# Weight loads on two queues at a written pace, K^T loads behind V, and a planner that lets instruction blocks wait for loads

## Chip, cores and metric

One core of one Trainium2 chip runs the kernel. The metric is the device time of a run in microseconds (us). Three runs of the kernel before gave 1008.52, 1013.25 and 1024.26 us (median 1013.25).

## What is computed

A delta-rule attention (4 batches, 8 heads, 768 positions, head size 48) feeds two mixture layers with 2048 hidden columns. Cut to what matters:

```python
k_n = k / (norm(k) + 1e-6)
for t in range(S):
    y[t]  = q[t] @ state
    v_old = k_n[t] @ state
    state = state + beta[t] * outer(k_n[t], v[t] - v_old)
h = x @ w_in;  g = P(h) / (Q(h) + 1e-6);  x = g @ w_out      # P cubic, Q quadratic in |h|
h = x @ w2_in; r = maximum(h, 0);         out = (r * r) @ w2_out
```

## The kernel before

The 768 positions are cut into 12 chunks of 64; a chunk of one batch is a step, eight steps are a group, and there are six groups. A group needs its Gram matrices (TensorE, line 583), the inverse of a triangular matrix, made row by row over 31 steps (lines 652 and 656: on VectorE for group 0, on GpSimd for the others), and then per step small matmuls (lines 793, 835, 841). The steps of group 0 are written apart: `halves` does the lower and upper 32 rows of a chunk (L835), with a cross product between them (L841), and `rest` makes outputs and the state (L793).

The 3072 tokens are cut into six tiles of 512. For every tile and each of 16 blocks of 128 hidden columns, `mm1` (L1128) makes h, `rational` the quotient, and `mm2_1` (L1216, or L1219 where the operands are split in two) adds g @ w_out. The second layer (`relu2`, `mm2_2`, L1249 to L1251) follows when all tiles are done. Tile 0 can start when group 0 has left its output; the later groups run between the matmuls of the tiles before.

The weights arrive as 768 KB blocks `src[j]`, 16 of them per layer, in 64-bit words. ScalarE (L1052, L1053), VectorE (L1069 to L1075) and again ScalarE, VectorE or GpSimd (L1086, L1088) turn each into 32-bit operands `A` and `B`. Blocks 0 to 3 land in `mem`, blocks 4, 5, 8 and later in two buffers `raw`, blocks 6 and 7 in `ra`. All loads are asked for by SyncE's queue (SP), from the helper `dma` (L399), in program order.

TensorE's clock is kept up early on by matmuls that compute nothing: `fill` (L513). A first run of six, one of 24 behind the first weight block (`gate`, L1064), and 13 spare ones of three that the planner sets where it thinks TensorE too idle.

What stands where is decided by a planner (`Plan`). Every piece of work is a task with an engine, a duration, a due time, and a time `nb` before which it is not started in the plan. `play` runs all tasks through a model of the engines, and `search` shakes the due times at random and keeps a set that brings more TensorE work forward. The finished order is then written out; the chip follows order and semaphores, and no time of the plan is in the program. So any change of a cost shifts the whole order, also where the cost does not apply.

The planner counts TensorE's instructions in blocks of 256 (`BLOCK`; `SENT` is where the count starts). When TensorE enters a block, the next one is fetched, and in the plan TensorE can't go into that one until a time `FETCH` later (L203):

```python
if e == "PE" and sent + t["ins"] > BLOCK:
    s = max(s, turn + FETCH[turn > 80] - t["dur"] * (BLOCK - sent) / t["ins"])
```

with `FETCH` 4.7 us up to 80 us of the plan and 3.0 us behind. A DMA occupies SP for `iss`, lands `lat` after its bytes have gone through at 240 KB per us (L254 to L257), and the program's semaphores let each DMA wait until the eighth one before it has landed.

## Time and profile before

| | |
|---|---|
| runs | 1008.52, 1013.25, 1024.26 us |
| the profiled execution | 1007.86 us |
| its span in the profile | 1006.1 us, so 1.8 us lie around it |
| TensorE busy | 972.7 us (97%) |
| VectorE, ScalarE, GpSimd busy | 676.8, 622.4, 498.8 us |
| granted TensorE clock, mean | 0.985 |

Line numbers (L1128) are those of the kernel. PE is TensorE's matmuls, SPq the DMA queue of SyncE; times start with the span. A row of the timeline has start, length, engine, line, operation and, in brackets, how long the engine sat idle before and what ended that. "issue" as the releaser means that the profile shows nothing that was waited for.

### The profile page before, as it was taken

How to read it: one execution, taken by the hardware profiler on the slowest of the kernel's cores; microseconds unless marked ns; L12 is line 12 of the kernel's file. 1: busy time of each engine (PE TensorE's matmuls, PEld its weight loads, DVE VectorE, ACT ScalarE, POOL GpSimd, SP SyncE). 2: the span in 40 equal slices, each digit the busy share in tenths (PEclk: the TensorE clock that was granted, in tenths of full speed). 3: DMA queues.
4: the chain of work that ended last, by engine and by line, in shares of the span. 5: the costliest groups of instructions: out<-in, count | busy, mean ns of one | idle time of the engine just before them, and what ended most of it. 6: DMA issues, size and time to landing. Idle time of an engine off the chain costs nothing.

```text
span 1006.1 us, 23661 instructions
## 1 busy us (share of the span) xinstructions
PE 972.7 (97%) x9682; PEld 776.1 (77%) x9682; DVE 676.8 (67%) x1097; ACT 622.4 (62%) x1129; POOL 498.8 (50%) x619
## 2 busy tenths in 40 slices
PE   5799999999989999999999999999999999999998
PEld 4678666678768778887888888888888888888886
DVE  7867877988897799779879998753333433334332
ACT  5557876988787688688769887652332333423322
POOL 4287389999999979975437977520000000000000
PEclk8779999999999999999999999999999999999999
DMA  7883875334343541333121227210010100000000
GB/s 195 235 261 99 166 227 132 85 78 122 77 100 78 150 102 47 83 95 58 29 77 53 69 94 288 94 53 11 1 64 0 32 32 1 32 1 1 32 1 32
DMA packets 127149, 85.14 MB, mean 85 GB/s; under 512 B 95616, under 2 KB 112000, under 8 KB 127040
## 3 DMA queue, kind: packets, MB, share of 16 engines
q1 hardware_dynamic: 127040, 83.62, 29.8%
q8 instruction: 76, 1.25, 0.5%
q14 instruction: 33, 0.27, 0.1%
HBM read 64.00 MB, written 18.61 MB: 82 GB/s over the span
## 4 chain that ended last, share of the span: by engine, by line
PE 77%; POOL 13%; DVE 5%; issue 2%; ACT 1%; DMA 1%; SPq 1%; POOLq 0%; DVEq 0%; ACTq 0%
PE bank L1128 33%; PE bank L1219 13%; PE bank L1251 7%; PE bank L1249 7%; PE bank L1250 7%; PE bank L793 6%; POOL mem L1167 3%; POOL Tt L656 3%; POOL tmp L652 3%; POOL pl L1190 2%; PE bank L1216 2%; PE bank L513 2%; DVE tmp L652 1%; DVE Tt L656 1%; SPq L399 1%
## 5 line engine op out<-in xcount | busy, mean ns | idle before, releaser
L1128 PE MATMUL bank<-xh,A 128*128 128x512 f32 (+1 forms) x1170 | 366.2, 395 | 3.1 <-DVE mem L1172 2.1
L1128 PEld LDWEIGHTS bank<-xh,A 128*128 128x128 f32 x1170 | 216.4, 188 | 57.2 <-issue 4.3
L1128 PE MATMUL bank<-xl,A 128*128 128x512 f32 (+1 forms) x585 | 226.5, 387 | 0.1
L1237 DVE SCALAR_TENSOR_TENSOR mem<-bank,mem 128x512 f32<-128x512 f32 x96 | 66.3, 691 | 159.3 <-ACT mem L1236 159.1
L1236 ACT ACTIVATE mem<-bank 128x512 f32<-128x512 f32 x96 | 57.4, 598 | 159.7 <-PE bank L1128 159.7
L1167 POOL TENSOR_TENSOR mem<-mem 128x512 f32<-128x512 f32 x89 | 116.3, 1308 | 53.0 <-ACT mem L1159 48.6
L1128 PEld LDWEIGHTS bank<-xl,A 128*128 128x128 f32 x585 | 109.9, 188 | 24.2 <-DVE xl L1112 0.9
L1251 PE MATMUL bank<-gh,C 128*128 128x512 f32 x288 | 113.7, 395 | 0.0
L1249 PE MATMUL bank<-gl,C 128*128 128x512 f32 x288 | 113.4, 394 | 0.0
L1190 POOL TENSOR_TENSOR pl<-mem,ph 128x512 fp32r<-128x512 f32 x78 | 102.6, 1315 | 21.3 <-ACT ph L1189 17.2
L1250 PE MATMUL bank<-gh,C 128*128 128x512 f32 x288 | 112.1, 389 | 0.0
L1240 DVE TENSOR_TENSOR gl<-mem,gh 128x512 fp32r<-128x512 f32 x96 | 69.2, 723 | 62.3 <-ACT gh L1239 62.3
L1219 PE MATMUL bank<-pl,E 128*128 128x512 f32 x240 | 97.5, 406 | 4.5 <-POOL pl L1190 4.1
L1239 ACT CAST gh<-mem 128x512 fp32r<-128x512 f32 x96 | 59.6, 621 | 67.0 <-DVE mem L1237 51.8
L656 POOL TENSOR_TENSOR Tt<-Tt,tmp 128x31 f32<-128x31 f32 (+15 forms) x155 | 91.8, 592 | 8.9
L1219 PE MATMUL bank<-ph,F 128*128 128x512 f32 x240 | 93.7, 391 | 0.0
L1219 PE MATMUL bank<-ph,E 128*128 128x512 f32 x240 | 93.6, 390 | 0.0
L652 POOL TENSOR_TENSOR tmp<-Gb,Tt 128x31 f32<-128x31 f32 (+15 forms) x155 | 87.6, 565 | 11.8 <-DVE Gb L629 2.2
L1179 ACT ACTIVATE mem<-mem,par 128x512 f32<-128x512 f32 x96 | 69.4, 723 | 31.3 <-POOL mem L1167 30.0
L1170 DVE SCALAR_TENSOR_TENSOR mem<-mem,par,bank 128x512 f32<-128x512 f32 x96 | 71.3, 742 | 20.2 <-ACT bank L1180 19.9
L1155 ACT ACTIVATE mem<-bank 128x512 f32<-128x512 f32 x96 | 56.7, 592 | 33.1 <-PE bank L1128 27.7
L1168 DVE TENSOR_TENSOR mem<-bank,mem 128x512 f32<-128x512 f32 x96 | 65.8, 686 | 12.9 <-ACT mem L414 7.2
(203 smaller groups left out, 1798.4 us busy)
## 6 DMA issues: line engine op xcount, KB each, us to landing
raw<-in_w_dram SPq DMA_DIRECT2D x17, 768.0 KB, 5.6
rb<-in_w_dram SPq DMA_DIRECT2D x8, 768.0 KB, 5.0
gs<-Gs SPq DMA_DIRECT2D x40, 128.0 KB, 2.5
X<-in_qT_dram SPq DMA_DIRECT2D x44, 112.0 KB, 2.9
kn<-in_kn_dram SPq DMA_DIRECT2D x12, 384.0 KB, 4.6
vn<-in_vn_dram SPq DMA_DIRECT2D x12, 384.0 KB, 3.4
y<-mem SPq DMA_DIRECT2D x18, 256.0 KB, 2.3
out_dram<-mem SPq DMA_DIRECT2D x18, 256.0 KB, 2.0
```

Source lines behind the costliest of these rows:

```text
L652: E_.tensor_tensor(tv, _mid(Gb[:, s, s + 1:32], [128, a, b]), Tt[:, 0:a, s:s + 1].to_broadcast([128, a, b]), op=ALU.mult)
L656: E_.tensor_tensor(Tt[:, 0:a, s + 1:32], Tt[:, 0:a, s + 1:32], tv, op=ALU.subtract if g else ALU.add)
L1128: M.matmul(h, a, b, start=(k == m == 0), stop=(k == NK - 1 and m == 2))
L1167: shared(1.29, 0.7, lambda E: E.tensor_tensor(b(), b(), a(), op=ALU.mult), r=[ak], w=[bk], due=due + 4.2)
L1170: q3 = lambda: V.scalar_tensor_tensor(c(), c(), s(0), h(), op0=ALU.add, op1=ALU.mult)
L1179: add("ACT", 0.72, lambda: A_.activation(a(), b(), AF.Ln, bias=s(6)), r=[bk, "par6"], w=[ak], due=due + 6)
L1190: shared(1.3, 0.7, lambda E: E.tensor_tensor(slot[mk][0], g(), slot[pk][0], op=ALU.subtract), r=[gk, pk], w=[mk], due=due + 11.5, alloc=(( ...
L1219: M.matmul(acc[d], a, b, start=(j == 0 and m == 0), stop=(j == NJ - 1 and m == 2))
L1240: add("DVE", 0.7, lambda: V.tensor_tensor(gl(), b(), gh(), op=ALU.subtract), r=[bk, gk, "late"], w=[lk], due=due + 5, lock=1, alloc=(("gl" ...
L1249: M.matmul(acc[d], wh, gl, start=(j == 0), stop=False)
L1250: M.matmul(acc[d], wl, gh, start=False, stop=False)
L1251: M.matmul(acc[d], wh, gh, start=False, stop=(j == NJ - 1))
```

## The change

Weight blocks 5 to 11 of the first layer are asked for by ScalarE's queue (`by=1`), blocks 5 to 10 at new times `PACE`. K^T of steps 8 to 11 stands behind the load of V of chunk 2 instead of a time of 55. K, V of chunk 2 and Q of steps 8 to 11 may start at 50 in the plan instead of 60. In the planner one `FETCH` of 2.7 us holds throughout, and the fetch of a block begins only when all loads asked for until then are drained in the model (`dma`). The threshold for spare fills becomes 3000 before 50 us of the plan and 1950 after it, instead of 2050. The other edits let a DMA stand on ScalarE's queue.

```diff
-BLOCK, SENT, FETCH = 256, 63, (4.7, 3.0)
+BLOCK, SENT, FETCH = 256, 63, 2.7
+QA, QB = 5, 12
+PACE = {5: 52.5, 6: 57.5, 7: 63, 8: 68, 9: 73, 10: 80}
-FILL0, FILLS, FILLN, LOOK, HOT, SPAN, SWAP = 6, 16, 3, 2.6, 2050, (41.5, 82), 0.08
+FILL0, FILLS, FILLN, LOOK, HOT, SPAN, SWAP = 6, 16, 3, 2.6, (3000, 1950), (41.5, 82), 0.08
-                s = max(s, turn + FETCH[turn > 80] - t["dur"] * (BLOCK - sent) / t["ins"])
+                s = max(s, turn + FETCH - t["dur"] * (BLOCK - sent) / t["ins"])
-            if e == "SP":
+            if t["kb"] or e == "SP":
                 free_at[e] = s + t["iss"]
...
                         turn = end - t["dur"] * sent / t["ins"]
+                        turn = max(turn + 0.3, dma)
-    def dma(kb, out, in_, r=(), w=(), due=0.0, lat=2.2, **kw):
+    def dma(kb, out, in_, r=(), w=(), due=0.0, lat=2.2, by=0, **kw):
         def go():
-            SY.dma_start(out() if callable(out) else out, in_() if callable(in_) else in_)
-        return add("SP", lat, go, r, w, due, kb=kb, **kw)
+            (SY, A_)[by].dma_start(out() if callable(out) else out, in_() if callable(in_) else in_)
+        return add(("SP", "ACT")[by], lat, go, r, w, due, kb=kb, **kw)
...
-                dma(384, VN[cb], vn[c], ..., nb=(16, 24, 60)[min(c, 2)], ...)
+                dma(384, VN[cb], vn[c], ..., nb=(16, 24, 50)[min(c, 2)], ...)
+                if c == 2:
+                    used["vn2"] = len(PL.tasks) - 1
-                dma(112, lambda: slot["kc", n][0:112], kT[n, 0:112], ..., nb=55 if n < 12 else 0, ...)
+                dma(112, lambda: slot["kc", n][0:112], kT[n, 0:112], ..., after=[used['vn2']] if n < 12 else [], ...)
...
-            nb=0 if l == 2 else WB + WS * j)
+            nb=0 if l == 2 else PACE[j] if j in PACE else WB + WS * j, by=int(l == 1 and QA <= j < QB), iss=0.45 if l == 1 and QA <= j < QB else 0.35)
```

In the order that comes of it nearly every row stands elsewhere. Three places are shown; the line numbers of the kernel after are 3 to 5 higher at the same code.

SP's queue at the start asks for the first K blocks: `TT1` is K^T of the first half-heads and `TT0` the same with the halves swapped. Before:

```order
L399 DMA TT1_125<-in_kT_dram 112x2x256
L399 DMA TT0_124<-in_kS_dram 112x2x256
L399 DMA TT1_125<-in_kT_dram 112x2x256
L399 DMA TT0_124<-in_kS_dram 112x2x256
L399 DMA be_136<-in_beta_dram 128x32
```

and after:

```order
L402 DMA TT1_125<-in_kT_dram 112x2x256 x2
L402 DMA TT0_124<-in_kS_dram 112x2x256 x2
L402 DMA be_136<-in_beta_dram 128x32
L1017 DMA par_82<-in_par_dram 128x6
L402 DMA TT1_125<-in_kT_dram 112x2x256
```

The second and third load have changed places, so the first pair is complete one load later. VectorE's copies out of the Gram matrices that these loads feed, before:

```order
L505 COPY TT0_124<-bank3_72 32x2x128 x4
L505 COPY TT0_124<-bank4_73 32x2x128 x4
L593 STREAM_TRANSPOSE Gb0_127<-TT0_124 128x1024
L858 TENSOR_TENSOR X0_120<-bank0_69,tri_135 128x4x64
L858 TENSOR_TENSOR X1_121<-bank1_70,tri_135 128x4x64
```

and after:

```order
L508 COPY TT0_124<-bank4_73 32x2x128 x3
L508 COPY TT0_124<-bank3_72 32x2x128 x4
L508 COPY TT0_124<-bank4_73 32x2x128
L598 STREAM_TRANSPOSE Gb0_127<-TT0_124 128x1024
L863 TENSOR_TENSOR X1_121<-bank1_70,tri_135 128x4x64
```

Now the first copies read bank 4, which belongs to the last of the four loads; before, they read bank 3 of the first pair.

SP's queue from weight block 4 on (`raw0`), before, with block 5 (`raw1`), K^T of steps 8 to 11 (`kTc`), block 6 (`ra2`) and Q (`X`):

```order
L399 DMA raw0_106<-in_w1_dram 128x768
L399 DMA raw1_107<-in_w1_dram 128x768
L399 DMA kTc0_145<-in_kT_dram 112x256
L399 DMA kTc1_146<-in_kT_dram 112x256
L399 DMA kTc2_147<-in_kT_dram 112x256
L399 DMA kTc3_148<-in_kT_dram 112x256
L399 DMA ra2_893<-in_w1_dram 128x768
L399 DMA X0_120<-in_qT_dram 112x4x64
```

and after:

```order
L402 DMA raw0_106<-in_w1_dram 128x768
L402 DMA X0_120<-in_qT_dram 112x4x64
L402 DMA X1_121<-in_qT_dram 112x4x64
L402 DMA X2_122<-in_qT_dram 112x4x64
L402 DMA vn0_143<-in_vn_dram 128x768
L402 DMA X3_123<-in_qT_dram 112x4x64
L402 DMA kn0_141<-in_kn_dram 128x768
L402 DMA kTc0_145<-in_kT_dram 112x256
```

Blocks 5 and 6 have left the queue, and what follows block 4 are loads into buffers that a step of group 0 must free first. The same blocks on ScalarE, after, where `XQ0` and `SX0` are the state that the first step left and `X1`, `UX1` copies of the second step's values:

```order
L417 CAST xh_100<-bank4_73 128x3x64
L417 COPY SX0_116<-bank5_74 112x3x16
L417 COPY XQ0_108<-bank5_74 112x4x48
L1091 CAST A2_86<-B0_177 128x384
L417 COPY UX1_113<-bank6_75 128x3x16
L417 COPY X1_121<-bank6_75 128x4x48
L402 DMA raw1_107<-in_w1_dram 128x768
L417 COPY UX2_114<-bank7_76 128x3x16
L417 COPY X2_122<-bank7_76 128x4x48
```

Block 5 now stands behind the copies of the first step's results, so it can't be asked for before TensorE has made these; before, it was asked for directly behind block 4.

## Rows read from the trace of the kernel before

**Rows 1.** The page: busy time of each engine (share of the span).

```profile
PE 972.7 (97%) x9682; PEld 776.1 (77%) x9682; DVE 676.8 (67%) x1097; ACT 622.4 (62%) x1129; POOL 498.8 (50%) x619
```

**Rows 2.** Stretches, all engines: PE, PEld, DVE, ACT, POOL busy, PEclk, DMA share, GB/s.

```profile
55.00:60.00 5.00, 2.84 (x22) 1.82 (x23) 2.56 (x6) 1.97 (x4) 4.37 (x9) 0.77 1.11 260
60.00:65.00 5.00, 5.00 (x67) 4.30 (x67) 2.86 (x6) 2.15 (x6) 4.53 (x7) 0.50 0.40 64
```

**Rows 3.** The chain that ended last, 50 to 80 us: start, length, what.

```profile
54.78 2.38 issue
57.16 1.27 PE bank L793 x17
58.43 1.57 PE bank L513 x3
60.01 0.78 PE bank L835 x16
60.79 1.02 PE bank L841 x16
61.81 1.69 PE bank L793 x16
...
65.85 1.49 PE bank L793 x31
...
68.23 0.46 PE bank L835 x16
68.69 0.91 PE bank L793 x16
69.61 0.89 PE bank L513 x3
...
71.76 1.51 PE bank L793 x48
...
74.63 0.60 PE bank L841 x16
```

**Rows 4.** Stretches from 0, PE alone: length, busy, matmuls, PEclk, DMA share, GB/s.

```profile
0.00:50.70 50.70, 33.67 (x598) 0.80 0.80 217
0.00:55.00 55.00, 37.74 (x726) 0.81 0.82 229
0.00:119.00 119.00, 98.80 (x1745) 0.87 0.70 190
```

**Rows 5.** Timeline of SP's queue, 48 to 54 us.

```profile
48.49 1.00 SPq L399 DMA_DIRECT2D raw<-in_w_dram  x2
49.53 2.47 SPq L399 DMA_DIRECT2D kTc<-in_kT_dram  x4
52.04 0.43 SPq L399 DMA_DIRECT2D ra<-in_w_dram  x1
```

**Rows 6.** DMA queues, 54.5 to 55 us: packets, MB, share of 16 engines.

```profile
DMA packets 139, 0.18 MB, mean 357 GB/s; under 512 B 20, under 2 KB 130, under 8 KB 138
...
q8 instruction: 1, 0.02, 12.2%
```

**Rows 7.** Timeline of TensorE, 5 to 45 us.

```profile
7.10 1.15 PE L491 MATMUL bank<-TT 48*64 48x64 f32 x60 [0.36 <-DMA TT<-in_kS_dram]
...
44.12 0.67 PE L841 MATMUL bank<-X,xin 32*64 32x48 f32 x16 [0.82 <-POOL A L1088]
```

**Rows 8.** Timeline of VectorE, 5 to 12 us.

```profile
6.65 3.47 DVE L505 COPY TT<-bank 32x256 f32<-32x256 f32 x8 [3.02 <-PE bank L491]
10.35 1.94 DVE L593 STREAM_TRANSPOSE Gb<-TT 128x1024 f32<-128x1024 f32 x1 [0.23 <-ACT TT L507]
```

**Rows 9.** What TensorE waited for from 84 us on: total, times, longest.

```profile
PE bank L1219 <- POOL pl L1190: 4.1, 6, 1.9
...
PE bank L793 <- issue: 1.1, 1, 1.1
PE bank L737 <- issue: 1.1, 1, 1.1
```

More of the change, by code (lines that the diff above doesn't have):

```diff
@@ L52 @@
 PORT = ("DVE", "POOL")
-AHEAD, FLOOR, RATE = 20, -1e9, dict(PE=1.0, DVE=0.1, ACT=0.1)
+AHEAD, RATE = 20, dict(PE=1.0, DVE=0.1, ACT=0.1)
 SEARCH = [(0, 60, 40), (40, 90, 40), (80, 130, 40), (120, 180, 40), (170, 230, 40), (220, 290, 40), (280, 350, 30), (340, 410, 30), (400, 470, 30), (460, 530, 30), (520, 620, 30)]
-BLOCK, SENT, FETCH = 256, 63, (4.7, 3.0)
+BLOCK, SENT, FETCH = 256, 63, 2.7
+QA, QB = 5, 12
+PACE = {5: 52.5, 6: 57.5, 7: 63, 8: 68, 9: 73, 10: 80}
 PREF, PREF2 = 1.0, 1.0
 IV1, WB, WS, GW = 30, 30, 4.5, 1.2
-FILL0, FILLS, FILLN, LOOK, HOT, SPAN, SWAP = 6, 16, 3, 2.6, 2050, (41.5, 82), 0.08
+FILL0, FILLS, FILLN, LOOK, HOT, SPAN, SWAP = 6, 16, 3, 2.6, (3000, 1950), (41.5, 82), 0.08
 WEIGH = dict(U1=96, P=96, U=96, H=448, Y=600, dS=192, G=256, GP=512, fl=512, h=2300)
@@ L107, in add @@
             t["alloc"] = alloc = [alloc]
-        if eng == "SP" and alloc:
+        if kb and alloc:
             t["pre"].update([self.last[alloc[0][0]]] if alloc[0][0] in self.last else [])
@@ L124, in run @@
             for s in t["suc"]:
-                t["due"] = min(t["due"], T[s]["due"] - 1.25 * t["dur"] - (2.4 if t["eng"] == "SP" else 0.1))
+                t["due"] = min(t["due"], T[s]["due"] - 1.25 * t["dur"] - (2.4 if t["kb"] or t["eng"] == "SP" else 0.1))
         due = self.search([t["due"] for t in T])
@@ L238, in play @@
                 hot = [y for y in hot if y[1] > x - LOOK]
-                if sum(y[2] * (y[1] - max(y[0], x - LOOK)) / (y[1] - y[0]) for y in hot) < HOT and x < s + 0.01:
+                if sum(y[2] * (y[1] - max(y[0], x - LOOK)) / (y[1] - y[0]) for y in hot) < HOT[x > 50] and x < s + 0.01:
                     s, i = x + SWAP * (not wide), spare.pop(0)
@@ L267, in play @@
                         turn = end - t["dur"] * sent / t["ins"]
+                        turn = max(turn + 0.3, dma)
             t["s"], t["e"] = s, end
-            if limit is not None and e in RATE and t["due"] > FLOOR:
+            if limit is not None and e in RATE and i not in self.spare:
                 work += RATE[e] * (min(end, limit) - s)
@@ L284, in play @@
                 n = T[k]
-                when[k] = max(when[k], (s if n["eng"] == e == "SP" and n["alloc"] and t["alloc"] else end) + (0 if n["eng"] == e and e != "SP" and not n["alt"] else 0.2 if n["eng"] == "PE" else 0.08))
+                when[k] = max(when[k], (s if n["kb"] and t["kb"] and n["alloc"] and t["alloc"] else end) + (0 if n["eng"] == e and e != "SP" and not n["alt"] else 0.2 if n["eng"] == "PE" else 0.08))
                 left[k] -= 1
@@ L551, in head @@
                 dl = dn - 14 if c > 1 else 6 + 10 * c
-                dma(384, KN[cb], kn[c], w=[("kn", cb)], due=dl, lat=2.2, nb=(16, 24, 60)[min(c, 2)], after=tailed if c in (2, 3) else [])
-                dma(384, VN[cb], vn[c], w=[("vn", cb, x) for x in range(B)], due=dl, lat=2.2, nb=(16, 24, 60)[min(c, 2)], after=tailed if c in (2, 3) else [])
+                dma(384, KN[cb], kn[c], w=[("kn", cb)], due=dl, lat=2.2, nb=(16, 24, 50)[min(c, 2)], after=tailed if c in (2, 3) else [])
+                dma(384, VN[cb], vn[c], w=[("vn", cb, x) for x in range(B)], due=dl, lat=2.2, nb=(16, 24, 50)[min(c, 2)], after=tailed if c in (2, 3) else [])
+                if c == 2:
+                    used["vn2"] = len(PL.tasks) - 1
                 def vs(E):
@@ L568, in head @@
             if n >= 8:
-                dma(112, lambda: slot["kc", n][0:112], kT[n, 0:112], w=[("kc", n)], due=dn - 4, nb=55 if n < 12 else 0, alloc=(("kTc",), ("kc", n)))
+                dma(112, lambda: slot["kc", n][0:112], kT[n, 0:112], w=[("kc", n)], due=dn - 4, after=[used['vn2']] if n < 12 else [], alloc=(("kTc",), ("kc", n)))
         def sb(n):
@@ L925, in result @@
             elif n < B:
-                dma(112, qS(n)[0:112, :, 0:64], qT[n + 2 * B], w=[("q", sb(n))], due=due + 25, iss=0.57, nb=60)
+                dma(112, qS(n)[0:112, :, 0:64], qT[n + 2 * B], w=[("q", sb(n))], due=due + 25, iss=0.57, nb=50)
             if b == B - 1 and not direct(n):
```

## The prediction

> **What bounds the kernel now.** I read the page first: TensorE is busy for 972.7 of 1006.1 us [rows 1], so only 33.4 us of its idle time can be won, and what its clock costs beside that. Next the stretches, to see where idle time and a low clock lie. From 55 to 60 us TensorE is busy for 2.84 of 5 us, and from 60 to 65 us it is busy throughout, at a granted clock of 0.50, the lower of its two levels [rows 2]. Third the chain of waits over that place. It shows 2.38 us of "issue" from 54.78 us on, and behind it only TensorE, piece upon piece [rows 3]. Each piece up to about 68 us is long against its like later on: three fills take 1.57 us and later 0.89, sixteen L835 take 0.78 and later 0.46. So the clock fell in or behind the gap and stayed down for some 11 us.
>
> What is "issue"? I counted the matmuls up to the gap: 726 [rows 4]. Another gap stands at 1745. The difference of 1019 is eight times 127.4, and a matmul is two instructions (the load of its weights and itself), so gaps stand at whole multiples of the planner's block of 256 instructions, give or take a branch. TensorE waited for its own code. One block ahead of 726 is matmul 598, reached at 50.70 us [rows 4]; entering that block asks for the next. SP had asked for two weight blocks at 48.49 us, four K^T blocks behind them and a third weight block at 52.04 us [rows 5]. The one packet of the instruction queue moved between 54.5 and 55 us, amid loads of 357 GB/s [rows 6], some 4 us after the block was entered; TensorE went on at 57.16 us. The loads held the code back. Ahead of this stage lies VectorE's inverse of group 0, a chain of single steps. Behind it TensorE has few gaps: its waits from 84 us on sum to some 10 us, 4.1 of them on GpSimd [rows 9]. What is saved before 85 us should therefore reach the end.
>
> **The change part by part.** The weight blocks: before, blocks 4, 5 and 6 were asked for within 4 us around the entry at 50.70 us. Now SP keeps block 4 alone, and the loads behind it wait for buffers of group 0's steps. Block 5 stands on ScalarE behind the casts and copies of the first step's results. I counted the matmuls ahead of those in the order: 596, so the block is entered (598) just as ScalarE gets to these six pieces, and only behind them is block 5 asked for. At the entry only block 4 is under way: 768 KB at 357 GB/s [rows 6] are 2.2 us, and it was asked for some 2.2 us earlier if that stays as before (48.49 to 50.70). So its bytes are through when the code is asked for, and I expect the code in time. That takes away 2.38 us [rows 3], and bounds are 0 and 2.38.
>
> With the gap the fall of the clock goes. Down to 67.3 us I set each piece of the chain against its like at the high clock [rows 3]: seventeen L793 1.27 against 0.97 (17/16 of 0.91), two groups of three fills 2 x (1.57 - 0.89), two groups of L835 2 x (0.78 - 0.46), L841 1.02 against 0.60, sixteen L793 1.69 against 0.91, thirty-one L793 1.49 against 0.98 (31/48 of 1.51). The sum is 0.30 + 1.36 + 0.64 + 0.42 + 0.78 + 0.51 = 4.0 us. This holds only if ScalarE and VectorE can follow; between 55 and 65 us they are busy for 4.1 and 5.4 of 10 us [rows 2], so there is room. Bounds 0 and 4.0.
>
> The start, which no edit names, moved as the whole search came out otherwise. The second and third load changed places, and VectorE's first copies now read a bank of the last load. Before, the matmuls of the first pair were done at about 6.65 us, where VectorE began its eight copies, 3.47 us [rows 8], while the second half waited for its load until 7.10 us [rows 7]. Now nothing can be copied before the second half is done: 7.10 + 64 matmuls at 1.15/60 us = 8.3 us, plus 3.47 = 11.8 us, where the transpose started at 10.35 us [rows 8]. The whole inverse of group 0 hangs on this. I take +1.4 us; bounds 0 (if the loads land earlier in their new order) and 1.7 (8.3 against 6.65).
>
> At 44.12 us TensorE's cross product had waited 0.82 us [rows 7]. Its operand is ScalarE's copy, which in the order before stands behind a cast that waited for VectorE; after, it stands ahead of it. I take -0.6 us; bounds -0.82 and 0.
>
> Seven requests on ScalarE: two on SP take 1.00 us, one 0.43 [rows 5], so 7 x 0.5 = 3.5 us over some 60 us. ScalarE has more than half its time free between 55 and 65 us [rows 2], so 0; if that cover failed at one place, 0.5 us each. K^T behind V: before, it was asked for at 49.53 us [rows 5] and first used behind the first matmuls of tile 0 in both orders; nothing waits, 0. Blocks 5 to 10 a few us later are wanted only by tile 0's later columns, 0. The lower `FETCH` and the new thresholds only reorder: both orders hold 6545 matmuls and 13 spare fills, so TensorE's work is equal. What another order does to the 10 us of gaps behind 84 us I can't read; I bound it by +4 and -4 us, the size of the waits on GpSimd [rows 9], and take 0.
>
> Sum: -2.4 - 4.0 + 1.4 - 0.6 = -5.6 us. Against the profiled execution, 1007.86 us (span 1006.1 and 1.8 around it), that gives 1002.3 us. The runs shown lie above it, the lowest by 0.7 us and the median by 5.4; I put the median of the kernel after 2.7 us above its sum, at 1005 us, which is 0.8% under the median before.
>
> **The rivals.** The gap moves. Two more code blocks are entered before 65 us, and V, K, K^T and block 7 now come together at about that time: some 2 MB behind blocks 5 and 6. If a code block is entered in that queue, TensorE waits again and the clock falls again. For it: the loads are the same bytes, only shifted. Against it: before, loads of the same size around 67 us caused no gap in the chain [rows 3]. Then only the terms of the start stay: 1007.9 + 1.4 - 0.6 = 1008.7 us, 1011 in the runs' terms.
>
> Two queues hold the code back longer. The trace shows that the code's one packet comes through late while one load queue is full [rows 6]. If code takes turns with the load queues, a second full queue makes it late by as much again, 4.8 us instead of 2.4. The place is the block entered next after 60 us, when SP's V and K and ScalarE's block 7 are both in flight; it decides once both have over 1 MB outstanding there. The price is 2.4 us more than the gap has now: 1008.7 + 2.4 = 1011.1 us, 1014 in the runs' terms: slower than before. For it: both queues do fill then. Against it: half the bytes stand in either. The Trainium skill says (DMA: Bandwidth & Descriptors, "Queues, rings and completion order") that each DMA engine goes round between the queue rows that have work, a packet at a time. By that rule this rival is right and the planner's rule of drained loads is not; the trace rather bears out the planner, since 4 us for one packet are far more than one turn.
>
> GpSimd takes the gain back. Its work gates TensorE by 4.1 us in six waits [rows 9]; if TensorE is earlier and GpSimd is not, these grow by as much as was won. For it: no other engine holds TensorE for as long there. Against it: GpSimd's work is itself released by tile 0's matmuls, so it starts earlier as well. Time: 1007.9 us, 1010 to 1011 in the runs' terms.
>
> More goes than I count: the two gaps of 1.1 us behind 84 us [rows 9] are of the same kind, and the planner now weighs loads there too. Then 1002.3 - 2.2 = 1000.1 us, 1003 in the runs' terms.
>
> **How the numbers follow.** I give my forecast 0.45, the moved gap 0.25, the two queues 0.1, GpSimd 0.12, the larger gain 0.08. The predicted time is 1005 us. Its own terms reach down by the 4 us of the unknown order and 2.2 of the other gaps, to 1000 less another 3 if the runs lie close to their profile: 996. Upward I take the two-queue case with the runs 5.4 us above the profile, 1011.1 + 5.4 = 1016.5, so 1016. A measurement tells about 2% (20 us) from no change. No case here is worth 20 us either way; what is left is an order that came out well or badly beyond all this: faster 0.03, within 2% 0.94, slower 0.03.
>
> **What would show it.** Right: no "issue" gap of TensorE between 50 and 60 us, a granted clock of 1.00 from 42 to 85 us, the first matmul of tile 0 some 5 to 6 us earlier, VectorE's first transpose at 11.5 to 12 us instead of 10.35, and ScalarE's request for block 5 behind matmul 598. Wrong: a gap of over 1.5 us anywhere before 85 us with a clock of 0.50 behind it, a first transpose at 10.4 us, ScalarE idle at a request, or waits on GpSimd from 160 to 380 us that grow by what was won.

## The result, and the profile after

In 22 runs of each the kernel after has a median of 1014.51 us (1009.51 to 1020.69) and the kernel before 1010.28 us (1004.87 to 1026.28). The ratio is 1.0053, with a 95% interval from 1.0033 to 1.0072: some 5 us slower, where 8 us less than 1013.25 was forecast. A second comparison (after_2 below) gave 1.0021 (0.9990 to 1.0052), and the kernel before against itself 0.9988 (0.9940 to 1.0037), so a ratio is good to some 0.2 to 0.5% and the loss is 2 to 5 us. Single runs of one kernel differ by up to 21 us, and the ratio leaves out runs over 1.5% above a kernel's fastest, which only before has here; over all 22 runs the means are 1013.0 us before and 1014.5 after, 1.5 us apart. The profiled execution of after has a span of 1010.5 us, 4.4 more than that of before.

The page of after, and its stretches from 55 to 65 us, all engines (the columns of [rows 2]); they answer to [rows 1, 2]:

```profile
PE 975.2 (96%) x9682; PEld 777.8 (77%) x9682; DVE 671.4 (66%) x1091; ACT 623.4 (62%) x1130; POOL 504.9 (50%) x624
```

```profile
55.00:60.00 5.00, 4.35 (x129) 3.38 (x127) 2.38 (x6) 2.77 (x10) 4.38 (x9) 1.00 1.08 282
60.00:65.00 5.00, 5.00 (x140) 4.06 (x140) 3.18 (x9) 2.98 (x7) 4.53 (x7) 1.00 0.74 241
```

TensorE is busy 4.35 and 5.00 us at a clock of 1.00, where it had 2.84 us, and 0.50 in the second stretch. So in this execution the middle went nearly as forecast. The timeline of TensorE, at four places (before, the gap was 2.38 us [rows 3]):

```profile
5.99 3.85 PE L494 MATMUL bank<-TT 48*64 48x64 f32 x124 [0.75 <-DMA TT<-in_kS_dram]
...
59.07 0.31 PE L798 MATMUL bank<-X 64*48 64x64 f32 x3 [0.65 <-issue]
...
123.50 0.67 PE L798 MATMUL bank<-vn,TT 64*64 64x48 f32 x16 [1.61 <-ACT TT L417]
...
281.07 1.22 PE L1133 MATMUL bank<-xh,A 128*128 128x512 f32 x2 [3.73 <-DVE mem L1177]
```

Of the gap 0.65 us is left, in front of the same line. The first row is the start: what stood as 60 matmuls in 1.15 us [rows 7], 19 ns each, is part of one row of 124 in 3.85 us, 31 ns each. VectorE, which answers to [rows 8]:

```profile
9.03 3.47 DVE L508 COPY TT<-bank 32x256 f32<-32x256 f32 x8 [5.40 <-PE bank L494]
12.61 1.95 DVE L598 STREAM_TRANSPOSE Gb<-TT 128x1024 f32<-128x1024 f32 x1
```

The copies begin at 9.03 instead of 6.65 us, the transpose at 12.61 instead of 10.35. How far TensorE has come is read from stretches that start at 0 (length, busy, matmuls, clock, DMA share, GB/s); before, and then after, with the ends chosen so that the counts match:

```profile
0.00:82.60 82.60, 63.19 (x1200) 0.81 0.75 214
0.00:110.90 110.90, 91.43 (x1500) 0.86 0.69 193
0.00:707.60 707.60, 677.66 (x8399) 0.98 0.41 112
```

```profile
0.00:79.10 79.10, 61.51 (x1200) 0.83 0.81 215
0.00:108.90 108.90, 91.15 (x1500) 0.87 0.73 196
0.00:712.00 712.00, 680.14 (x8399) 0.98 0.42 112
```

The first 1200 matmuls take 82.6 us before and 79.1 after: a lead of 3.5 us. At 1500 it is 2.0 us, and at 8400 after is behind by 4.4. The table gives the start of the matmul with that number in every kernel, minus the same of before's first profile. Where the matmuls stand in before's order (b_spread_2, b_spread_late, before_2, and b_tail up to 1500) the numbers compare like with like. In the other rows long and short matmuls are mixed otherwise, and a number there can be off by some 3 us: after, which leads by 3.5 at 1200 and 2.0 at 1500, stands at +1.3 at 1400.

| matmuls | 500 | 1200 | 1500 | 2000 | 2500 | 8400 |
|---|---|---|---|---|---|---|
| after | +2.4 | -3.5 | -2.0 | +3.0 | +4.7 | +4.4 |
| b_spread_2 | +1.0 | -4.4 | -2.6 | -0.6 | -0.4 | +0.2 |
| b_spread_late | 0.0 | -4.0 | -1.0 | -1.5 | -1.0 | -1.5 |
| b_mid | +0.2 | -5.9 | -4.4 | +0.1 | -1.2 | -0.4 |
| b_tail | -0.1 | -4.3 | -3.6 | +3.6 | +4.8 | +3.6 |
| a_start | -0.3 | -4.7 | -3.6 | +4.0 | +5.2 | +3.8 |
| a_scal | +0.6 | -4.6 | -2.4 | +2.1 | +4.0 | +2.8 |
| a_all | +0.4 | -5.6 | -4.0 | +0.8 | +2.0 | +1.8 |
| a_sp | +2.4 | -3.2 | -1.9 | +5.8 | +6.9 | +5.1 |
| a_burst | +2.9 | +5.2 | +6.3 | +12.3 | +13.5 | +11.8 |
| before_2 | 0.0 | +10.1 | +10.3 | +10.1 | +10.4 | +10.3 |
| after_2 | +2.1 | +5.2 | +6.3 | +9.4 | +11.5 | +10.6 |

What TensorE waited for from 84 us on (total, times, longest) answers to [rows 9]:

```profile
PE bank L1133 <- DVE mem L1177: 4.0, 2, 3.7
PE bank L1224 <- POOL pl L1195: 2.7, 5, 1.1
PE bank L798 <- ACT TT L417: 2.2, 2, 1.6
PE bank L1133 <- DVE xl L1117: 2.2, 2, 1.6
```

GpSimd's product, 4.1 us before, fell to 2.7. The wait for L1177 (L1172 there) grew from 2.1 us in all to 4.0, and two waits of 2.2 us came up. The largest, at 281 us, can be followed back through three engines. GpSimd, ScalarE, VectorE, and then the stretches of TensorE alone behind it:

```profile
275.13 2.28 POOL L1172 TENSOR_TENSOR mem<-mem 128x512 f32<-128x512 f32 x1
```

```profile
277.44 0.72 ACT L1184 ACTIVATE mem<-mem,par 128x512 f32<-128x512 f32 x1 [4.05 <-POOL mem L1172]
```

```profile
278.83 0.75 DVE L1175 SCALAR_TENSOR_TENSOR mem<-mem,par,bank 128x512 f32<-128x512 f32 x1 [2.57 <-ACT bank L1185]
```

```profile
280.00:284.00 4.00, 2.93 (x7) 0.53 0.00 0
284.00:288.00 4.00, 4.00 (x12) 0.62 0.00 0
```

L1172 on GpSimd stands in its order behind four row steps of another inverse. Its operand was ready at 271.15 us, it began at 275.13 and took 2.28 us (1.30 elsewhere), beside a VectorE step of 1.62 us (L634). ScalarE waited 4.05 us for it, VectorE 2.57 for ScalarE, TensorE 3.73 for VectorE, and then the clock was 0.53 and 0.62 for two stretches. At 123 us it is alike: ScalarE waits until 121.44 us for a load that L603 needs, and the copies for which TensorE waits stand behind and start at 122.29 us:

```profile
121.44 0.35 ACT L603 ACTIVATE tmp<-Gb,tiny 128x32 f32<-128x32 f32 x1 [2.99 <-DMA Gb<-gs]
```

### The profile page after: what moved, and what is told of

Read it like the earlier page. It is cut to its first block, busy times and chain, and to the rows that moved or that the text cites. A ratio compares the mean times of both kernels' runs of the same rounds, so it can differ in the third digit from the quotient of the medians.

```text
span 1010.5 us, 23663 instructions
## 1 busy us (share of the span) xinstructions
PE 975.2 (96%) x9682; PEld 777.8 (77%) x9682; DVE 671.4 (66%) x1091; ACT 623.4 (62%) x1130; POOL 504.9 (50%) x624
## 4 chain that ended last, share of the span: by engine, by line
PE 66%; POOL 13%; DVE 3%; ACT 2%; issue 1%; DMA 1%; SPq 0%; POOLq 0%; DVEq 0%; ACTq 0%
PE bank L1133 30%; PE bank L1224 11%; PE bank L1256 7%; PE bank L1254 7%; PE bank L1255 6%; PE bank L798 4%; POOL Tt L661 3%; POOL tmp L657 3%; POOL mem L1172 3%; POOL pl L1195 2%; POOL A L1093 1%; DVE mem L1175 1%; DVE mem L1177 1%; PE bank L730 0%; DVE bank L1176 0%
## 5 line engine op out<-in xcount | busy, mean ns | idle before, releaser
L1172 POOL TENSOR_TENSOR mem<-mem 128x512 f32<-128x512 f32 x89 | 116.8, 1313 | 46.2 <-ACT mem L1164 44.0
L657 POOL TENSOR_TENSOR tmp<-Gb,Tt 128x31 f32<-128x31 f32 (+15 forms) x155 | 83.3, 537 | 11.1 <-DVE Gb L634 1.3
```

The lines of the kernel that those rows point to most:

```text
L657: E_.tensor_tensor(tv, _mid(Gb[:, s, s + 1:32], [128, a, b]), Tt[:, 0:a, s:s + 1].to_broadcast([128, a, b]), op=ALU.mult)
L1172: shared(1.29, 0.7, lambda E: E.tensor_tensor(b(), b(), a(), op=ALU.mult), r=[ak], w=[bk], due=due + 4.2)
```

## The experiments

Most kernels hold an order fixed. The search is replaced, and the order is a list of task numbers put together from the two orders, with single tasks moved; buffers follow.

```diff
-        due = self.search([t["due"] for t in T])
...
-        self.order = best[1]
+        self.order = ORDER
```

A ratio is to the kernel before on the same chip. Names that begin with a_ hold the order of after, with b_ that of before, and what is mixed is said.

**The requests alone: b_spread.** Only these rows move (on SP, the four K^T rows stand behind V instead):

```diff
 L1091 CAST A2_86<-B0_177 128x384
+L402 DMA raw1_107<-in_w1_dram 128x768
 L1091 CAST A3_87<-mem_102 128x384
...
 L1058 ACTIVATE raw1_107<-raw1_107 128x768
+L402 DMA ra2_912<-in_w1_dram 128x768
```

> The order of the kernel before, frozen, with six requests moved and nothing else: weight block 5 on ScalarE behind the third block's cast (about 53 us), block 6 on ScalarE behind block 5's first cast, K^T of steps 8 to 11 on SP behind V. Theory: the gap of 2.4 us at 54.8 us goes and with it the clock of 0.50 behind it, 6.4 us are won by 85 us, and as the rest of the order is that of before they reach the end: 1004 us, a ratio of 0.994 to before. Rival A (requests on ScalarE cost, or the casts of block 5 come late): 1009 to 1012 us. Rival B (the stage from 160 us on takes the gain back): the lead is there at 85 us and gone by 380 us, 1009 to 1010 us.

0.9951 (0.9917 to 0.9985). The profiled execution took 1021.10 us. The gap is there, longer than in before, and TensorE is at 0.50 until some 94 us:

```profile
58.41 0.26 PE L798 MATMUL bank<-X 64*48 64x64 f32 x1 [2.98 <-issue]
```

The next run is the same kernel once more.

> The same kernel as b_spread again, for a profile that is not disturbed: theory: no gap of over 0.7 us between 50 and 60 us, granted clock 1.00 from 42 to 85 us, TensorE 5 to 6 us ahead of the kernel before at 85 us and at the end; 1004 to 1006 us. Rival B: the lead at 85 us is gone by 380 us. Rival A: block 5's casts are late and TensorE waits for weights of tile 0.

0.9960 (0.9908 to 1.0012). TensorE in three stretches, and its row behind the gap:

```profile
55.00:60.00 5.00, 3.99 (x101) 1.00 0.38 142
60.00:65.00 5.00, 5.00 (x123) 1.00 0.85 285
65.00:80.00 15.00, 14.87 (x352) 1.00 0.66 227
```

```profile
56.82 0.21 PE L798 MATMUL bank<-X 64*48 64x64 f32 x1 [1.01 <-issue]
```

In this execution a gap of 1.01 us is left (0.7 was the bound), the clock is 1.00 throughout, and the lead at 1200 matmuls is 4.4 us. By the ratios 4 to 5 us reach the end, though the interval of the second runs past 1, and rival A falls. But that the requests remove the gap is not shown: it was 1.01, 2.98 and, in b_spread_late below, 2.48 us with them moved, 2.38 and 1.83 us (before_2) without. What SP's queue (q1) moved from 50 us until the code's packet came, in before and in b_spread_late (packets, MB, share of 16 engines):

```profile
q1 hardware_dynamic: 631, 1.74, 97.9%
```

```profile
q1 hardware_dynamic: 1532, 1.40, 102.3%
```

Blocks 5 and 6 and K^T had left SP's queue, Q of steps 8 to 11 had moved up behind block 4, and the engines were as full as before. Matmul 598 was reached at 50.7 us in both, and the code's packet came between 54 and 54.5 us, where it was 54.5 to 55. That the loads hold the code back agrees with this; that it is the loads which were moved does not.

In the profile of b_spread_2 the lead is 2.6 us at 1500, 0.6 at 2000 and gone at the end. ScalarE and SP at the first of these places:

```profile
96.23 2.03 ACT L686 COPY Gb<-Tt 128x1024 f32<-128x1024 f32 x1 [2.54 <-POOL Tt L661]
```

```profile
98.29 0.77 SPq L402 DMA_DIRECT2D nd<-Gb  x2
```

L686 copies the inverse of group 1, whose row steps (two instructions each) stand on GpSimd from 50.34 to 96.20 us, 45.9 us; in before they take 45.4 us, in after 46.9. In before ScalarE came to that copy (L681 there) at 97.98 us, 3.3 us behind the last row step (94.72), and did not wait. Now it waits 2.54 us, with steps of tile 0 behind it in its order, and TensorE waits 0.25 and 1.20 us between 99 and 102 us. Between 1500 and 2000 matmuls the lead falls by another 2.0 us, with a gap without a wait of 1.55 us at 117.23 us (1.08 in before) and a clock of 0.85 and 0.80 from 115 to 125 us.

**That copy later: b_spread_late.**

```diff
+L1184 ACTIVATE mem_102<-mem_102,par_82 128x512
+L1185 ACTIVATE bank5_74<-mem_102 128x512
+L1160 ACTIVATE mem_102<-bank4_73 128x512
+L1164 ACTIVATE mem_102<-mem_102,par_82 128x512 x2
 L686 COPY Gb1_128<-Tt1_130 128x1024
-L1184 ACTIVATE mem_102<-mem_102,par_82 128x512
...
```

> b_spread with one more move: ScalarE's transposing copy of group 1's inverse (L686) and the two stores that follow it behind the five steps of tile 0 that stood behind it; nothing else. Theory F (the row steps of group 1's inverse on GpSimd, 49 to 96 us, do not get faster with the loads; ScalarE reaches the copy 2.5 us ahead of the inverse's end and holds up tile 0 behind it, so most of the lead of 4.8 us is given back there): ScalarE's wait of 2.5 us at 96.2 us is gone, TensorE's wait of 1.2 us at 101.7 us too, and the lead at matmul 1500 is 3 to 5 us instead of 0.8: 1003 to 1005 us, ratio 0.991 to 0.994. Rival G (the lead is lost at the code gaps and the clock's fall between 100 and 125 us, not at the inverse): the wait goes, the lead at matmul 1900 is under 1 us as before, ratio 0.995 to 0.997.

0.9952 (0.9919 to 0.9985), the same as b_spread and where rival G had put it. The lead is 4.0 us at 1200, 1.0 at 1500 and 1.5 at the end. The gap at 57 us, of which the expectation said nothing, is 2.48 us. ScalarE's wait at 96.2 us is gone, but what TensorE waits for has only changed:

```profile
57.22 0.21 PE L798 MATMUL bank<-X 64*48 64x64 f32 x1 [2.48 <-issue]
...
102.18 0.72 PE L1133 MATMUL bank<-xh,A 128*128 128x512 f32 x2 [1.09 <-ACT Gs L417]
...
106.12 0.68 PE L588 MATMUL bank<-kTg 48*64 48x64 f32 x16 [0.73 <-DMA kTg<-in_kS_dram]
```

```profile
101.22 0.77 SPq L402 DMA_DIRECT2D nd<-Gb  x2
```

The stores of the inverse (`nd`) left SP at 101.22 instead of 98.29 us, and the K blocks for which TensorE now waits twice (0.73 us, and 0.76 at 107.56 us) stand behind them in SP's queue. Theory F's price is wrong. Nor is it rival G's reason here: the clock is 1.00 from 85 to 130 us, and the lead goes ahead of 1500 matmuls, where these three waits sum to 2.58 us. That other queues waiting for the same inverse are the wall is argued from these rows and not shown. The one kernel in which the inverse ends earlier, b_mid_best below (93.56 us against 95.49 in b_mid), came out no better, though its profile has another wait ahead of that place.

**The same with the burst put back: a_burst.** On SP, after's order:

```diff
 L402 DMA raw0_106<-in_w1_dram 128x768
+L402 DMA raw1_107<-in_w1_dram 128x768
+L402 DMA kTc0_145<-in_kT_dram 112x256
...
+L402 DMA ra2_707<-in_w1_dram 128x768
 L402 DMA X0_120<-in_qT_dram 112x4x64
```

> The order of the kernel after, frozen, with weight blocks 5 and 6 and K^T of steps 8 to 11 asked for on SP directly behind block 4, as in the kernel before, and the other blocks on SP at the places where ScalarE asked for them. Theory: a gap of 2 to 3 us without a wait comes back on TensorE at 57 to 60 us, with a clock of 0.50 behind it, and the kernel loses 5 to 6 us: 1020 us. Rival C (the gap of before came from its order of matmuls, not from when the loads were asked for): no gap, 1014.5 us.

1.0079 (1.0040 to 1.0119), median 1019.62 us where 1020 was forecast, but not in the shape of the forecast. There is no long gap, as rival C had said; TensorE waits 1.32 us at 57.15 us behind a cast that waits for block 3 (its load took 8.8 us), 0.72 us at 68.23 for code, and the clock is 0.66 from 65 to 80 us. That early requests cost by holding up whatever load is in flight is one reading; the next run has the same loss without the burst, so it is not shown.

**SP's queue at the later places: a_sp.** `QA, QB = 12, 12` in after's order, so no block is on ScalarE.

> The order of the kernel after, frozen, but blocks 5 to 11 asked for by SP at the same places of the order: SP's queue is in program order, so a request there stands behind the loads that wait for buffers. Theory (ScalarE's seven requests cost nothing): within 1.5 us of the kernel after, 1013 to 1016 us. Rival A (the requests on ScalarE cost 0.5 us each or hold up its copies): 1010 to 1012 us, with TensorE's waits for ScalarE from 50 to 125 us smaller.

1.0083 (1.0051 to 1.0115), median 1016.87 us: not better than after, and 0.9 us over the theory's upper bound. So ScalarE's requests cost nothing that shows, and rival A falls here too. In the profile ScalarE waits 2.43 us for a weight block at 126.17 us and TensorE 3.45 us at 127.62, which after does not have; SP's queue seems to bring that block later, which is argued. The gap before 59.37 us is 0.34 us with block 5 asked for at 52.78 us. As the gap varies by execution (a_pool below), this does not tell pace from queue. And a_sp, with paced requests, is as slow as a_burst with early ones: both have no block on ScalarE's queue.

**The start: a_start.** The first 221 tasks in before's order; on SP:

```diff
-L402 DMA TT1_125<-in_kT_dram 112x2x256 x2
-L402 DMA TT0_124<-in_kS_dram 112x2x256 x2
+L402 DMA TT1_125<-in_kT_dram 112x2x256
+L402 DMA TT0_124<-in_kS_dram 112x2x256
+L402 DMA TT1_125<-in_kT_dram 112x2x256
+L402 DMA TT0_124<-in_kS_dram 112x2x256
```

> The order of the kernel after, frozen, with its first 221 tasks in the order of the kernel before (the loads, copies and row steps of group 0 up to about 40 us); everything behind them as in the kernel after. Theory (the edits do what they should between 42 and 85 us, the order that came out with them costs at the start and again behind 85 us): the first transpose at 10.4 us instead of 12.6, the inverse of group 0 2.1 us earlier, the matmuls up to 85 us 2 to 3 us earlier, still no gap at 50 to 60 us, and the wait of 3.7 us at 281 us still there; 1012 us, about 2.3 us under the kernel after. Rival A (the requests on ScalarE and the paced loads are what costs): no change, 1014.5 us. Rival B (from 160 us on GpSimd sets the pace and takes back whatever is won): the lead is there at 85 us and gone by 380 us, 1014.5 us.

1.0021 (0.9991 to 1.0052). The transpose starts at 11.01 us, and the lag of 2.4 us at 500 matmuls is gone; at 1200 it is 1.2 us ahead of after, at 2000 no longer. Against the two ratios of after this is not told apart.

**The place at 281 us: a_pool.** On GpSimd (and L634 on VectorE behind L1177):

```diff
+L1172 TENSOR_TENSOR mem_102<-mem_102 128x512
 L657 TENSOR_TENSOR tmp1_132<-Gb1_128,Tt1_130 128x207
...
-L1172 TENSOR_TENSOR mem_102<-mem_102 128x512
```

> The order of the kernel after, frozen, with one product of tile 1's last block (L1172) moved on GpSimd ahead of four row steps of the next inverse, directly behind its operand, and the step L634 of VectorE behind the same block's last product; nothing else. Theory: ScalarE's wait of 4.05 us and TensorE's of 3.73 us at 281 us shrink to under 1.2 us, the granted clock from 280 to 288 us is 1.00 instead of 0.53 to 0.62, and 4 to 7 us are won: 1008 to 1010 us. Rival B (GpSimd is the bound there, so a piece moved forward pushes another back): TensorE waits as long a little later, 1013 to 1015 us. Rival A (the loads' side costs): no change, 1014.5 us.

1.0003 (0.9971 to 1.0035), median 1012.91 us: by the ratio 2 to 5 us under after, by the median just under rival B's 1013. The waits at the place are 1.86 and 2.90 us, as in a_all below. Up to 272 us this is the order of after, and in this execution (1023.97 us) the gap near 60 us is as long as in before, with a clock of 0.54 from 60 to 65 us and 0.50 from 65 to 80:

```profile
60.01 0.26 PE L798 MATMUL bank<-X 64*48 64x64 f32 x2 [2.55 <-issue]
```

That is the sign which the prediction had named for being wrong.

**The place at 123 us: a_scal.** On ScalarE:

```diff
+L417 COPY TT1_125<-bank7_76 32x16x32 x3
 L603 ACTIVATE tmp0_131<-Gb0_127,tiny_133 128x32
 L604 ACTIVATE nbr_137<-tmp0_131,par_82 128x32
 L607 ACTIVATE tmp0_131<-tmp0_131 128x32
-L417 COPY TT1_125<-bank7_76 32x16x32 x3
```

> The order of the kernel after, frozen, with the three norm steps of group 2 (L603, L604, L607) on ScalarE, which wait there for a load until 121.4 us, moved behind the three copies of group 1's inverse (L417) that stood behind them and were ready at about 118.3 us; with them VectorE's L614 to L616. Theory (waits that the new order brought cost, each by itself): TensorE's wait of 1.6 us for these copies at 123.5 us goes, 1.6 us are won, 1013 us. Rival B (what is won ahead of 160 us is taken back): the wait goes and the end stays, 1014.5 us.

1.0010 (0.9969 to 1.0050). The wait of 1.61 us is gone, and the next one grew from 0.92 to 2.23 us:

```profile
125.25 0.70 PE L1133 MATMUL bank<-xh,A 128*128 128x512 f32 x2 [2.23 <-ACT Gs L417]
```

The lag at 2000 is 2.1 us instead of 3.0. In the profile the wait moved, as rival B says; the ratio is too wide to say more.

**All three: a_all.**

> The order of the kernel after with three repairs together: the first 221 tasks as in the kernel before, the move on GpSimd and VectorE at 272 us of a_pool, and the move of a_scal. Theory: the three add up, 2.5 to 3 us from the start, 4 to 5 us from the place at 281 us and 1.6 us from the one at 123 us: 1004 to 1006 us, a ratio of 0.995 to before, under both kernels. Rival B (the stage from 160 us on, where GpSimd is busy throughout, takes back what is won ahead of it): only the place at 281 us counts, 1009 to 1010 us. Rival A (requests on ScalarE cost): the same, 1009 to 1010 us.

0.9976 (0.9941 to 1.0012), median 1009.47 us: about 8 us under after's first ratio, whose interval it does not touch, 5 under its second, whose interval it overlaps. The median is where rivals A and B had put it, above the 1004 to 1006 us of the theory, whose ratio of 0.995 the interval includes. The lag at the end is 1.8 us instead of 4.4. TensorE around the place at 281 us:

```profile
272.24 0.50 PE L1133 MATMUL bank<-xl,A 128*128 128x512 f32 x1 [1.88 <-DVE xl L1117]
...
282.48 1.22 PE L1133 MATMUL bank<-xh,A 128*128 128x512 f32 x2 [2.86 <-DVE mem L1177]
```

The wait for L1117 grew from 1.55 to 1.88 us, that for L1177 shrank from 3.73 to 2.86, and there the clock fell all the same (0.71 and 0.50 in the two stretches). So the repairs won less than their waits. On GpSimd the next product now stands behind row steps, which is argued as the reason.

**Pieces of both orders.** b_mid has before's first 221 tasks, after's up to 625 (about 110 us), then before's; b_tail before's first 625 and then after's; b_mid_best is b_mid with three moves, of which the one on GpSimd is

```diff
-L562 TENSOR_TENSOR vn1_144<-vn1_144,nT1_139 128x768
...
 L661 TENSOR_TENSOR Tt1_130<-Tt1_130,tmp1_132 128x31
+L562 TENSOR_TENSOR vn1_144<-vn1_144,nT1_139 128x768
```

> The first 221 tasks in the order of the kernel before, then the order of the kernel after up to its task 625 (about 110 us), then the rest in the order of the kernel before. Theory: the start of before, the middle of after without gap and with the high clock, and the tail of before without the wait at 281 us: 1003 to 1005 us, under both kernels. Rival A (the loads' side costs): 1010 us or more. Rival B (the stage from 160 us on takes the gain back): 1009 to 1010 us, a lead at 85 us that is gone by 380 us.

0.9965 (0.9931 to 0.9999), median 1008.03 us, between the theory and rival B. A lead of 5.9 us at 1200; at 122.74 us TensorE waits 3.17 us for ScalarE, and at 2000 nothing is left. This run and a_start were made on one chip and have one order up to task 625; behind it b_mid has before's order and a_start after's. Their ratios are 0.9965 and 1.0021, their medians 1008.03 and 1011.45 us. So after's order behind 110 us costs some 3 to 6 us, the cleanest reading of that term here; the two intervals overlap by 0.0008.

> The kernel before up to its task 625 (about 110 us), then the order of the kernel after; block 11 is on ScalarE in the latter. Theory: the later part of the new order is what costs, without any of the edits' effect ahead of it: the waits at 123 us and at 281 us with the clock's fall behind the latter appear, 5 to 7 us slower than before, a ratio of 1.005 to 1.007. Rival D (the loss of the kernel after lies ahead of 110 us, and waits behind that only show it): as before, 0.999 to 1.001.

1.0010 (0.9969 to 1.0051): at rival D's upper bound, but the interval reaches the theory's lower one. Contrary to what was written, blocks 5 to 10 too were on ScalarE here, at before's places, so its first part is not before's. Its profile has a lead of 4.3 us at 1200, then waits of 2.34 us at 123.52 and 3.71 us at 280.50 us, and ends 3.6 us behind: behind 1500 matmuls the order of after lost 7.2 us here and before's order in b_mid 4.0.

> b_mid (start of before, middle of after, tail of before) with three moves: V's product (L562) on GpSimd behind group 1's inverse instead of in its middle, L686 on ScalarE behind four steps of tile 0, and group 2's norm steps (L603 to L607) on ScalarE behind the copies that they held up at 120 us. Theory F: the inverse ends 1.8 us earlier, at 93.5 us, ScalarE does not wait for it, TensorE's wait of 3.2 us at 122.7 us and the clock of 0.66 behind it are gone: 1001 to 1004 us, ratio 0.989 to 0.993, the best of all. Rival B: no better than b_mid, 0.996 to 0.998, as the stage from 160 us on takes it back.

0.9984 (0.9954 to 1.0014): no better than b_mid. The inverse ended at 93.56 us, as forecast. The profile has another wait (1.91 us for ScalarE at 50.04 us) and a fall of the clock ahead of 85 us, so what the earlier end was worth can't be read from it.

**Other seeds of the search.** `random.Random(2)` and `random.Random(3)` instead of `random.Random(1)`, in either kernel.

> The kernel before with another seed of its planner's search (2 instead of 1): the same rules, another order. Theory (the rules are worth a few us, the order that the search happens to find as much again): a ratio anywhere from 0.993 to 1.007, a gap without a wait of 2 us or so at 54 to 58 us. Rival E (the search finds orders of equal worth, so the seed does not matter): 0.998 to 1.002.

1.0097 (1.0061 to 1.0133).

> The kernel after with seed 2. Theory: no gap of over 1 us without a wait at 50 to 62 us and a granted clock of 1.00 there, as with seed 1; the end anywhere from 0.990 to 1.006 of the kernel before, as the waits at 123 and 281 us belong to the order of seed 1. Rival E (the seed does not matter, the rules themselves cost): 1.004 to 1.007, as with seed 1.

1.0031 (1.0003 to 1.0059). Besides the gap shown below, its profile has one of 1.19 us at 73.07 us.

> The kernel before with seed 3 of its search. Theory (the order that the search happens to find is worth as much as the edits): anywhere from 0.997 to 1.012, with a gap of about 2 us without a wait at 54 to 63 us. Rival E (seed 2 was an exception): 0.998 to 1.002.

1.0070 (1.0034 to 1.0105).

> The kernel after with seed 3. Theory: no gap of over 1 us without a wait at 50 to 63 us; under the kernel before of the same seed by 3 to 6 us, as with seed 2 (1.0031 against 1.0097). Rival E (the edits make the kernel slower whatever the seed, as with seed 1): 3 to 6 us over the kernel before of the same seed.

1.0008 (0.9978 to 1.0037). With 1.45 us the gap is over the bound of 1 us here. TensorE's row behind the gap in each of the four, in this order:

```profile
62.41 0.23 PE L793 MATMUL bank<-X,kn 64*48 64x48 f32 x1 [2.62 <-issue]
```

```profile
56.64 0.49 PE L840 MATMUL bank<-vn,Gb 32*32 32x48 f32 x14 [0.19 <-issue]
```

```profile
57.13 0.64 PE L793 MATMUL bank<-XQ,TT 48*64 48x112 f32 x9 [2.33 <-issue]
```

```profile
56.94 0.39 PE L516 MATMUL bank<-A 128*128 128x512 f32 x1 [1.45 <-issue]
```

At these seeds after is 6.7 and 6.3 us faster than before (differences of the ratios, 0.0066 and 0.0062, times 1010 us), at seed 1 some 2 to 5 us slower. Before's own orders spread over 10 us, and seed 1 is its best by 7; after's spread over 2 to 5 us. So rival E falls both ways: the changed planner is better at two seeds of three, and at seed 1 it trades an order that had come out well for one that had not. How much of this is the edits and how much the draw, three seeds can't tell.

**Both kernels once more.**

> The kernel before once more, as any other kernel: how far a ratio strays where nothing is changed, and whether the gap and the clock's fall of its first profile belong to the kernel or to one execution. Theory (the gap comes from the loads, the fall behind it only in some executions): ratio 0.997 to 1.003; a gap of 1 to 3 us without a wait at 55 to 58 us again, the granted clock of 42 to 85 us either near 0.88, as in the first profile, or at 1.00 with TensorE 4 to 5 us further at matmul 1000. Rival (both belong to the kernel): gap and 0.88 again.

0.9988 (0.9940 to 1.0037). A gap of 1.83 us came, as the theory said; the clock from 42 to 85 us was 0.70, lower than either value that it had named.

> The kernel after once more, beside the kernel before on the same chip. Theory (its loss lies in the order found): ratio 1.003 to 1.007 again; no gap of over 1 us at 50 to 62 us; the waits at 123 us (1.6 us) and at 281 us (3.7 us) again, as they belong to the order; the clock's fall behind the latter may be there or not. Rival (the ratio of 1.0053 came from one chip): 0.998 to 1.002.

1.0021 (0.9990 to 1.0052), between the theory and the rival, with the wait of 3.73 us at 287.01 us again, and that for copies at 123 us only 0.6 us. TensorE in stretches, before_2 and then after_2:

```profile
55.00:60.00 5.00, 3.17 (x51) 0.88 1.07 283
60.00:65.00 5.00, 5.00 (x61) 0.50 0.91 152
65.00:80.00 15.00, 15.00 (x234) 0.50 0.51 202
```

```profile
55.00:60.00 5.00, 4.30 (x135) 1.00 0.98 256
60.00:65.00 5.00, 5.00 (x77) 0.61 0.59 192
65.00:80.00 15.00, 15.00 (x226) 0.50 0.45 137
```

The fall of the clock is there in both, for about 34 and 20 us, behind gaps of 1.83 and 0.70 us. The row behind the gap in after_2:

```profile
58.83 0.31 PE L798 MATMUL bank<-X 64*48 64x64 f32 x3 [0.70 <-issue]
```

Before's first profile had the fall for some 10 us, b_spread_late not at all, behind 2.48 us:

```profile
60.00:65.00 5.00, 5.00 (x129) 1.00 0.83 262
```

It belongs to the execution. before_2 is 10.1 us behind at 1200 and 10.3 us at 8400. Some 24 us more at the low clock cost it 10.1 us, so by an estimate from these two profiles the 10 us of the first cost some 4.2: the prediction's 4.0 was right in size for that execution.

## Why the prediction was wrong

Three steps failed: "What is saved before 85 us should therefore reach the end", "What another order does to the 10 us of gaps behind 84 us I can't read; I bound it by +4 and -4 us [...] and take 0", and "With the gap the fall of the clock goes". Step by step:

- The gap, -2.4: 0.65 us left in after and 0.70 in after_2, so -1.7, but 2.55 in a_pool, which is the same up to 272 us; the rival of the moved gap named such a return, with the clock's fall. "At the entry only block 4 is under way" was wrong: the prediction, as the section on the change, let the Q loads wait for buffers, but in after SP asked for three of them from 52.17 us on, directly behind block 4 (51.67), and the block of code was entered at 53.5 us. What held the code back in before stays open: with blocks 5 and 6 and K^T moved away, the gap came in full in two profiles of three. At two other seeds 0.2 and 1.4 us are left, against 2.6 and 2.3 before.
- The clock, -4.0: right in size for before's first profile, wrong as a term. The fall does not go with the gap: it stayed away behind 2.48 us (b_spread_late) and came behind 0.70 us (after_2). Falls of 0, 10, 34 and (b_spread) 36 us were seen for before's order of matmuls, and of 0, 20 and (a_pool) 24 us for after's. An expected value needed more than one profile.
- The start, +1.4: undersized; the transpose came 2.3 us later, outside the bound of 1.7. The price was taken from a row at 19 ns a matmul, and the 124 matmuls ran at 31 ns. By 1200 matmuls 1.2 us of it counted (a_start against after).
- The wait at 44.12 us, -0.6, and the requests, 0: nothing speaks against them; a_sp, without ScalarE's requests, is not faster.
- Up to 85 us the sum was -5.6 and came out as -3.5. That it came near is luck: without the 4.0 us of clock that before's execution lost and after's did not, no lead would stand there.
- That it reaches the end: the lead fell from 3.5 us at 1200 matmuls to 2.0 at 1500, and from 4.4 to 2.6 and then 0.6 at 2000 in b_spread_2, where nothing else was moved. Group 1's inverse on GpSimd ended at 97.80 us in after (94.72 before); its first row step came 1.6 us later and L562 stood in its midst for 1.8. ScalarE and SP wait for it in order. The rival on GpSimd may have named the right engine, at the wrong place (160 to 380 us); that is argued. By its ratio b_spread does keep 4 to 5 us, though its three profiles (with b_spread_late) end 13.2 us behind, 0.2 behind and 1.5 ahead of before's first. What that gain is made of stays open.
- The order behind, 0: from -2.0 at 1500 to +4.4 at 8400, 6.4 us in the profile, beyond the bound of 4; 3 to 6 us by b_mid against a_start. The rows at 123 and 281 us are where it shows; a_all wins back 5 to 8 us. What each of its three repairs is worth is not settled, as waits moved when they were taken away singly. I had bounded this term by the waits that before has. The seeds show what it should have been bounded by: orders of before's rules differ by 7 to 10 us, and the one in hand was the best of three.

The rival of the two queues was not tested. Behind 60 us, the place that it named, TensorE of after shows no gap without a wait until 110 us; but its condition was not met, as the queues moved their bytes one after the other (from 62 to 64 us 0.65 MB on ScalarE's and 0.05 on SP's, from 64 to 66 us 0.02 and 0.45). The Trainium skill (DMA: Bandwidth & Descriptors, "Queues, rings and completion order") lets each DMA engine go round between queue rows, and by that rule a second full row should delay the code; no run here shows it. How long such a turn lasts stands in no row either, so that 4 us are "far more than one turn" was not shown.

b_spread, at 0.9951 and 0.9960, and b_spread_late, at 0.9952, have before's order with the requests moved and lie under both kernels, though the interval of the second number runs past 1.

## What to carry to other kernels

Where a change runs through a seeded search, its effect is that of the edit plus that of a new draw; hold the order fixed and apply the edit alone before judging it, or time a few seeds of both. A lead of one engine is worth only as much as the slack in the in-order queues of the others: look for the long chain that it does not speed up (here probably an inverse on GpSimd) and for who waits for that chain in front of other work. A stretch at the low clock in one profile should not go into a sum at full size without a second profile, and neither should a gap that lasted from 0.65 to 2.55 us under one order.

## What the runs showed of the hardware

The fall of TensorE's clock to 0.50 (1.2 GHz) was not fixed by the gap ahead of it: a gap of 2.48 us was followed by 1.00 (b_spread_late), one of 0.70 us by 20 us near 0.50 (after_2). At 0.50 it stayed while TensorE was busy for 15.00 of 15 us (before_2, 65 to 80 us). The Trainium skill (TensorE: Matmul & The Clock Gate, "Part 1: The HAM clock gate") says that the same kernel shows different numbers of matmuls at the low clock from run to run at its start, and that sustained work brings the high clock back. Here a stretch in mid-kernel differed too, and the trace does not agree with the second: the engine worked some 34 us at the low clock, mostly on small matmuls, before it rose (before_2).

In before's order a lag from such a fall was carried to the end whole (before_2, 10.3 us at 1500 matmuls and at 8400). In after's it was not: after_2 is 8.7 us behind after at 1200 and 6.3 at 8400. Leads of 3 to 6 us at 1200 shrank in all profiles of the table.

The gap without a wait near 57 to 60 us, read as TensorE waiting for its own code, was 1.83 to 2.38 us in two executions of before, 1.01 to 2.98 us in three with six requests moved, and 0.65 to 2.55 us in three of after's order up to there.
